# Attention scores of the later chunks as two full-array float32r products in place of one 64-row float32 product

## The chip, the cores and the metric

The kernel runs on one core of one Trainium2 chip. Times are device microseconds from launch to end; a kernel is judged by the median of several runs. The profiler takes one execution instruction by instruction, and its span runs from the first to the last instruction.

## What is computed

Banded attention with sink tokens, followed by a two-layer feed-forward block. The reference, cut to what matters (B=4, H=8, S=768, D=64, n_sink=4, window=128; the feed-forward block has 512 inputs and 2048 inner units):

```python
scores = scale * np.matmul(q, k.transpose(0, 1, 3, 2))
keep = is_sink | in_window            # the first 4 keys, or the last 128
scores = np.where(keep, scores, -1000000000.0)
a = np.exp(scores - np.max(scores, axis=-1, keepdims=True))
a = a / (np.sum(a, axis=-1, keepdims=True) + 1e-09)
x = np.matmul(a, v)                   # heads side by side: 3072 rows of 512
h = x @ w_in
sp = np.where(h > 20.0, h, np.log1p(np.exp(np.minimum(h, 20.0))))
g = h * np.tanh(sp)
y = g @ w_out
```

## The kernel before

The 3072 rows are cut into 12 chunks of 256 rows (two blocks of 128 queries). The four chunks that open a batch see one or two blocks of keys and come first; the other eight, the late chunks, see three blocks of keys, of which each query block uses two and 32 columns of sinks, 288 columns in all.

Attention of a chunk goes by pairs of heads (`pair`). The two heads of a pair lie on the two halves of the 128 partitions, each with its 64 dimensions as rows: `ks` holds k and `qh` holds q, transposed. For each of the two query blocks `qk` makes the scores, one float32 product for each head (L358), with 64 rows of contraction each, in PSUM tiles `att`. VectorE (DVE) adds the mask and takes the minimum (L365), ScalarE (ACT) exponentiates (L368), the sums give `rc` (L371 to L373), the rows are normalised on ACT (L379) or DVE (L378), TensorE (PE) transposes them (L389, L398 for the sinks), copies bring them to SBUF (`pth`, `psk`, `sks`), and PE multiplies them with v (L407, 64 output columns for each head, and L411 for the sinks). The result is split into a float32r part and a float32r rest (`w`).

The feed-forward block goes by steps, eight for each chunk and 96 in all (`step`). A step takes two of the 16 blocks of inner units: 24 products of 256 columns (L446, tile `hp`; each float32 product is made of three float32r products of high and low parts), a chain on ACT and DVE (L454 to L459), a copy to the high part `gh` (L247) and a subtraction for the low part `gl` (L258 on GpSimd, which the profile calls POOL, or L260 on DVE), and 12 products of 512 columns (L474, tile `acc`; eight read `gh`, four `gl`). The weights come as float64 and are split into float32r parts by DVE, ACT and POOL in the first 190 us.

The order of every engine's instructions is fixed beforehand. Each piece of work is added to a plan with a rank, a price on each engine that can do it, and the buffers that it takes; `solve` lets the plan run in a model and picks engine and place, and `emit` writes the instructions in that order. Where the model leaves PE without work, `emit` puts products of zeros (L569). Copies go to ACT or DVE (`copy_ways`), subtractions to POOL or DVE (`sub_ways`), loads to SyncE's queue, SP (`load`). Buffers have tags with a number of places: `raw` 3 (the weights as they come), `w` 81, `ks` and `qh` 2 each.

Of the kernel before, what the change touches and what calls it, by code (L numbers as in the profile page):

```python
# [14 lines left out]
F32R = mybir.dt.float32r  # L15
# [6 lines left out]
B, H, S, D = 4, 8, 768, 64  # L22
DM, DF = 512, 2048
P = 128
NBLK = S // P
SK = 32
PITCH = P + SK
# [4 lines left out]
TB = 2  # L32
T = TB * P
# [7 lines left out]
PE, ACT, DVE, POOL, SP = "pe", "act", "dve", "pool", "sp"  # L41
# [8 lines left out]
LEAD, LEADG, LEADN = 11, (20, 14, 8), 9  # L50
WARM, SPARE, ROOM = 14, 250, 4
ZERO = 224
SH, QUICK = 1.0, 2
LOWS = {"wi": "dpppdpdddddddddd", "wo": "dppppppppppddddd"}


def f32(ap):
    return ap.bitcast(F32)
# [19 lines left out]
def pe_t(*ns):  # L78
    return sum(n / 2.4 + 13.3 for n in ns)
# [24 lines left out]
class Plan:  # L104
# [6 lines left out]
    def add(self, prio, ways, deps=(), bufs=(), new=()):  # L111
        deps = {id(d): d for d in list(deps) + [b.maker for b in bufs] if d is not None}
        t = Task(prio, ways, list(deps.values()), list(bufs) + list(new), list(new))
        for b in t.bufs:
            b.users += 1
        for b in new:
            b.maker = t
        self.tasks.append(t)
        return t
# [104 lines left out]
class Fast(Base):  # L224
# [82 lines left out]
    def operands(self, b, c3, pr, rank, pre):  # L307

        i0 = TB * c3
        first = c3 == 0  # L310
        nb = 2 if first else 3
        j0 = 0 if first else i0 - 1
        w = nb * PITCH - SK
        if pre:
            ks, qh, vt = (Buf(None, None) for _ in range(3))
            ks.t, qh.t, vt.t = pre
            return (ks, qh, vt, [], []), None, []
        ks, qh, vt = Buf("ks", [P, 3 * PITCH - SK]), Buf("qh", [P, T]), Buf("vt", [P, 2, 3, D])
        hs = slice(2 * pr, 2 * pr + 2)
        ldk = [self.load(rank, ks, lambda: ks.t[:, 0:w], self.k[b, pr, :, j0 * PITCH:j0 * PITCH + w], w / 2),  # L320
               self.load(rank, qh, lambda: qh.t, self.q[b, pr, :, i0 * P:i0 * P + T], T / 2)]
        ldv = [self.load(rank + 1, vt, lambda: vt.t[:, :, 0:nb, :], self.v[b, hs, :, j0:j0 + nb, :].rearrange("h p j d -> p h j d"), nb * 64)]
        if first:
            return (ks, qh, vt, ldk, ldv), None, []
        vr = Buf("vsr", [P, TB, P])
        return (ks, qh, vt, ldk, ldv), vr, [self.load(rank + 1, vr, lambda: vr.t, self.vs[b, pr], 128)]

    def pair(self, b, c3, pr, rank, x, x_done):


        nc, add = self.nc, self.plan.add
        first = c3 == 0
# [6 lines left out]
        for i in range(TB):  # L339
            r = rank + i  # L340
            nm, sm, rc = Buf("nm", [P, 2]), Buf("sm", [P, 2]), Buf("rc", [P, 2])
            if not first:
                n, mask, c0 = W2, self.m2, i * PITCH
            elif i == 0:
                n, mask, c0 = P, self.m0, 0
            else:
                n, mask, c0 = 2 * P, self.m1, 0
            st = [Buf("att", [P, n]) for _ in range(2)]

            def mov(rows, n=n, c0=c0):  # L350
                if n == 2 * P:
                    return ks.t[rows, 0:2 * PITCH].rearrange("p (a c) -> p a c", c=PITCH)[:, :, 0:P]
                return ks.t[rows, c0:c0 + n]

            def qk(st=st, mov=mov, i=i):
                for e in range(2):
                    rows = slice(e * D, (e + 1) * D)
                    yield nc.tensor.matmul(st[e].t, qh.t[rows, i * P:(i + 1) * P], mov(rows), start=True, stop=True)  # L358
            s = add(r, {PE: (2 * (n / 1.2 + 106) + 100, qk)}, ldk, [ks, qh], st)
            ex = []  # L360
            for e in range(2):
                new = ([p2] if i == 0 else []) + [nm, sm] if e == 0 else []
# [2 lines left out]
                a = add(r + .03 + .01 * e, {DVE: (dve_t(n) + 8, lambda st=st, pv=pv, nm=nm, e=e, mask=mask, n=n: nc.vector.tensor_tensor_reduce(  # L365
                    out=pv(), in0=st[e].t[:, 0:n], in1=mask, scale=-0.125, scalar=BIG, op0=ALU.add, op1=ALU.min, accum_out=nm.t[:, e:e + 1]))},
                    [s], [st[e]] + old, new)
                a = add(r + .05 + .01 * e, {ACT: (act_t(n, ptr=2), lambda pv=pv, nm=nm, sm=sm, e=e: nc.scalar.activation(  # L368
                    pv(), pv(), AF.Exp, bias=nm.t[:, e:e + 1], scale=-1.0, accum_out=sm.t[:, e:e + 1]))}, [a], [p2, nm, sm])
                ex.append(a)  # L370
            a = add(r + .07, {ACT: (act_t(2), lambda rc=rc, sm=sm: nc.scalar.activation(rc.t, sm.t, AF.Copy, bias=1e-9), 0, PEN_N),  # L371
                              DVE: (72, lambda rc=rc, sm=sm: nc.vector.tensor_scalar(rc.t, sm.t, 1e-9, None, ALU.add))}, ex, [sm], [rc])
            a = add(r + .08, {DVE: (84, lambda rc=rc: nc.vector.reciprocal(rc.t, rc.t))}, [a], [rc])  # L373
# [9 lines left out]
            cols = (0, PITCH) if not first else ((None, 0) if i == 0 else (0, P))  # L383
# [6 lines left out]
            a = add(r + OTP, {PE: (109 * (2 if cols[0] is None else 4), tr)}, norm, [p2], [pt])  # L390
# [4 lines left out]
        if not first:  # L395
            psk = Buf("psk", [P, 2 * TB, SK])
            a = add(rank + 1.11, self.copy_ways(P, lambda: psk.t, lambda: p2.t.rearrange("p i e c -> p (i e) c")[:, :, P:PITCH]), norms, [p2], [psk])
            a = add(rank + OTP + 1.02, {PE: (109, lambda: nc.tensor.transpose(ssk.t, psk.t.rearrange("p a c -> p (a c)"), self.ident))}, [a], [psk], [ssk])  # L398
            last.append(add(rank + OTP + 1.09, self.copy_ways(P, lambda: sks.t, lambda: ssk.t, True), [a], [ssk], [sks]))
        r = rank + TB + OVP  # L400
# [439 lines left out]
```

## Time and profile before

| | |
|---|---|
| median of 3 runs | 762.6 us (762.48 to 765.71) |
| the profiled execution | 764.29 us, its span 762.5 us |
| busy PE / ACT / DVE / POOL | 746.5 / 553.6 / 418.4 / 111.7 us |
| granted TensorE clock | 0.995 on the mean |
| moved by DMA | 52.62 MB |

Busy is the time in which an engine has an instruction running; for PE this takes in loading and emptying between two products, so a full PE is not yet a PE at its peak. A float32 product shows as two records, a float32r product as one. The share of an engine is an average over stages: in the first 190 us ACT and DVE split weights, later they serve attention and the chain of the steps alone.

### The profile page before, as it was taken

Reading aid. Unit: us, or ns where it says so; the run is one execution under the profiler, and the core shown is the slowest. Engines: PE = TensorE matmul, PEld = TensorE weight load, DVE = VectorE, ACT = ScalarE, POOL = GpSimd, SP = SyncE. Lnnn points to the kernel's source line nnn. Section 1 sums busy time; section 2 is a strip of 40 time slices with the busy share of each in tenths; the row PEclk is TensorE's granted clock in tenths of the full one; section 3 lists DMA queues with packets and bytes.
Section 4 is the critical chain, followed back from the end, with each engine's and each line's share of the span. In section 5 each row is a group of like instructions: output and inputs, shape, how many; then the busy total and the mean of one; then the engine's idle time right before and its main releaser. Section 6 shows DMA issues by size and latency. Waiting matters only on the chain.

```text
span 762.5 us, 13564 instructions
## 1 busy us (share of the span) xinstructions
PE 746.5 (98%) x5042; PEld 618.1 (81%) x5042; DVE 418.4 (55%) x1195; ACT 553.6 (73%) x1224; POOL 111.7 (15%) x91
## 2 busy tenths in 40 slices
PE   7989999999999999999999999999999999999996
PEld 5767888788878778887788888888887888788995
DVE  6899999997555544355543434343444434443322
ACT  5899998787675677766667777777777777775653
POOL 0454422221100002100000211111021112020000
PEclk9999999999999999999999999999999999999998
DMA  6554344440221113112212212111211311100000
GB/s 191 162 162 130 119 129 129 121 120 8 85 83 49 37 46 93 37 37 73 66 37 64 62 48 65 37 57 54 65 37 41 97 37 37 65 18 1 28 1 33
DMA packets 39771, 52.62 MB, mean 69 GB/s; under 512 B 3856, under 2 KB 32528, under 8 KB 39696
## 3 DMA queue, kind: packets, MB, share of 16 engines
q1 hardware_dynamic: 39696, 51.66, 22.4%
q8 instruction: 42, 0.69, 0.4%
q14 instruction: 33, 0.27, 0.1%
HBM read 45.35 MB, written 6.29 MB: 68 GB/s over the span
## 4 chain that ended last, share of the span: by engine, by line
PE 80%; ACT 11%; DVE 4%; DMA 2%; issue 1%; ACTq 0%; DVEq 0%
PE acc L474 30%; PE hp L446 30%; PE att L358 6%; PE att L407 5%; PE att L389 4%; PE att L411 3%; ACT p L368 2%; PE att L446 2%; ACT p L379 1%; ACT w L247 1%; ACT w L279 1%; DMA raw<-w_out 1%; ACT pth L247 1%; ACT u L458 1%; ACT u L457 1%; ACT u L456 1%
## 5 line engine op out<-in xcount | busy, mean ns | idle before, releaser
L446 PE MATMUL hp<-w,w 128*128 128x256 f32 x2208 | 302.5, 288 | 0.8 <-DVE n L459 0.6
L446 PEld LDWEIGHTS hp<-w,w 128*128 128x128 f32 x2208 | 277.2, 191 | 17.8 <-issue 11.4
L474 PE MATMUL acc<-w,gh 128*128 128x512 f32 x768 | 198.8, 396 | 0.0
L474 PEld LDWEIGHTS acc<-w,gh 128*128 128x128 f32 x768 | 136.4, 189 | 29.1 <-issue 5.9
L258 POOL TENSOR_TENSOR gl<-n,gh 128x512 fp32r<-128x512 f32 x46 | 59.4, 1292 | 445.5 <-ACT gh L247 371.3
L459 DVE SCALAR_TENSOR_TENSOR n<-u,hp 128x512 f32<-128x512 f32 x92 | 62.8, 684 | 98.4 <-ACT u L458 98.1
L455 DVE TENSOR_SCALAR u<-u 128x512 f32<-128x512 f32 x96 | 41.6, 433 | 124.2 <-ACT u L454 124.1
L474 PE MATMUL acc<-w,gl 128*128 128x512 f32 x384 | 107.9, 395 | 0.0
L368 ACT ACTIVATE p<-p,nm 128x288 f32<-128x288 f32 (+1 forms) x192 | 95.2, 497 | 16.7 <-DVE nm L365 16.7
L247 ACT ACTIVATE gh<-n 128x512 fp32r<-128x512 f32 x94 | 59.3, 631 | 54.3 <-DVE n L459 54.1
L456 ACT ACTIVATE u<-u,bias 128x512 f32<-128x512 f32 x96 | 69.3, 723 | 38.8 <-DVE u L455 38.8
L454 ACT ACTIVATE u<-hp 128x512 f32<-128x512 f32 x92 | 54.7, 595 | 46.1 <-PE hp L446 44.1
L474 PEld LDWEIGHTS acc<-w,gl 128*128 128x128 f32 x384 | 70.8, 188 | 14.3 <-DVE gl L260 0.3
L365 DVE CUSTOM_DVE_ANT_0 p<-att,m 128x288 f32<-128x288 f32 (+1 forms) x192 | 74.6, 419 | 2.9 <-PE att L358 1.7
L457 ACT ACTIVATE u<-u,bias 128x512 f32<-128x512 f32 x96 | 69.0, 720 | 2.2
L358 PE MATMUL att<-ks,qh 64*128 64x288 f32 (+2 forms) x376 | 66.6, 431 | 0.0
L379 ACT ACTIVATE p<-p,rc 128x288 f32<-128x288 f32 (+2 forms) x105 | 50.4, 497 | 19.1 <-DVE rc L373 19.1
L389 PE MATMUL att<-ident,p 128*128 128x128 f32 x352 | 56.0, 276 | 5.5 <-ACT p L379 2.0
L458 ACT ACTIVATE u<-u 128x512 f32<-128x512 f32 x96 | 59.9, 625 | 1.7
L358 PEld LDWEIGHTS att<-ks,qh 64*128 64x128 f32 x376 | 28.5, 186 | 27.7 <-issue 24.2
L389 PEld LDWEIGHTS att<-ident,p 128*128 128x128 f32 x352 | 41.2, 140 | 11.1 <-ACT p L379 3.6
L260 DVE TENSOR_TENSOR gl<-n,gh 128x512 fp32r<-128x512 f32 x50 | 36.3, 727 | 22.9 <-PE acc L474 12.7
(78 smaller groups left out, 664.7 us busy)
## 6 DMA issues: line engine op xcount, KB each, us to landing
raw<-w_in SPq DMA_DIRECT2D x16, 512.0 KB, 3.7
raw<-w_out SPq DMA_DIRECT2D x16, 512.0 KB, 4.2
ks<-k_p SPq DMA_DIRECT2D x32, 224.0 KB, 2.5
y<-u SPq DMA_DIRECT2D x24, 256.0 KB, 2.1
vt<-v_b SPq DMA_DIRECT2D x32, 192.0 KB, 3.3
qh<-q_p SPq DMA_DIRECT2D x47, 128.0 KB, 2.5
vsr<-v_s SPq DMA_DIRECT2D x32, 128.0 KB, 3.0
ks<-k_p SPq DMA_DIRECT2D x15, 144.0 KB, 2.1
```

The source lines that it names most:

```text
L247: ways[ACT] = act_t(n, psum), lambda: nc.scalar.activation(dst(), src(), AF.Copy, scale=scale or 1.0)
L258: ways[POOL] = pool_t(n), lambda: nc.gpsimd.tensor_tensor(dst(), a(), b(), ALU.subtract)
L358: yield nc.tensor.matmul(st[e].t, qh.t[rows, i * P:(i + 1) * P], mov(rows), start=True, stop=True)
L365: a = add(r + .03 + .01 * e, {DVE: (dve_t(n) + 8, lambda st=st, pv=pv, nm=nm, e=e, mask=mask, n=n: nc.vector.tensor_tensor_reduce(out=pv() ...
L368: a = add(r + .05 + .01 * e, {ACT: (act_t(n, ptr=2), lambda pv=pv, nm=nm, sm=sm, e=e: nc.scalar.activation(pv(), pv(), AF.Exp, bias=nm.t[: ...
L389: yield nc.tensor.transpose(pt.t[:, e, x * P:(x + 1) * P], p2.t[:, i, e, cols[x]:cols[x] + P], self.ident)
L446: yield nc.tensor.matmul(hp.t[:, y, :], w_.t[:, fs], x_.t[:, kt % 2, :], start=kt == 0 and n_ == 0, stop=kt == KT - 1 and n_ == 2)
L456: a = add(r + .52, {ACT: (act_t(N, ptr=1), lambda: nc.scalar.activation(u.t, u.t, AF.Square, bias=self.one))}, [a], [u])
L457: a = add(r + .53, {ACT: (act_t(N, ptr=1), lambda: nc.scalar.activation(u.t, u.t, AF.Ln, bias=self.half, scale=0.5))}, [a], [u])
L458: a = add(r + .54, {ACT: (act_t(N), lambda: nc.scalar.activation(u.t, u.t, AF.Exp, scale=-1.0))}, [a], [u])
L459: e = add(r + .55, {DVE: (dve_t(N), lambda: nc.vector.scalar_tensor_tensor(m.t, u.t, 1.0, hp.t, ALU.subtract, ALU.mult))}, [a], [u, hp], [m])
L474: yield nc.tensor.matmul(acc[t].t, g_.t[:, y, ts_], w_.t, start=new and n_ == 0, stop=done)
```

## The change

In the late chunks (`not first`) the scores are made from float32r parts. A new function, `halves`, loads k of each head twice, once onto partitions 0 to 63 and once onto 64 to 127, with the two heads side by side in the columns (tile `raw`, 2 x 448 columns), and q in the same way (tile `w`, 2 x 256 columns). A copy rounds k to float32r on all 128 partitions; a subtraction puts the rest of k on the lower 64. For q a copy makes the rounded part `qa` and a subtraction the rest `qb`, both on all 128 partitions. So one product of `qa` with `ks` over 128 rows holds two of the four terms, one of `qb` with `ks` the other two, and they add up in PSUM: two products for each head, four for each query block. Loads have rank 3 below the pair's, as before; the splitting comes 1.5 later (`SPL`).

```diff
--- before.py
+++ after.py
@@ -50,6 +50,7 @@
 LEAD, LEADG, LEADN = 11, (20, 14, 8), 9
 WARM, SPARE, ROOM = 14, 250, 4
 ZERO = 224
+SPL = 1.5
 SH, QUICK = 1.0, 2
 LOWS = {"wi": "dpppdpdddddddddd", "wo": "dppppppppppddddd"}
 
@@ -315,15 +316,40 @@
             ks, qh, vt = (Buf(None, None) for _ in range(3))
             ks.t, qh.t, vt.t = pre
             return (ks, qh, vt, [], []), None, []
-        ks, qh, vt = Buf("ks", [P, 3 * PITCH - SK]), Buf("qh", [P, T]), Buf("vt", [P, 2, 3, D])
+        vt = Buf("vt", [P, 2, 3, D])
         hs = slice(2 * pr, 2 * pr + 2)
+        if not first:
+            vr = Buf("vsr", [P, TB, P])
+            ks, qh, deps = self.halves(b, j0, i0, w, pr, rank)
+            ldv = [self.load(rank + 1, vt, lambda: vt.t, self.v[b, hs, :, j0:j0 + nb, :].rearrange("h p j d -> p h j d"), nb * 64)]
+            return (ks, qh, vt, deps, ldv), vr, [self.load(rank + 1, vr, lambda: vr.t, self.vs[b, pr], 128)]
+        ks, qh = Buf("ks", [P, 2 * PITCH]), Buf("qh", [P, T])
         ldk = [self.load(rank, ks, lambda: ks.t[:, 0:w], self.k[b, pr, :, j0 * PITCH:j0 * PITCH + w], w / 2),
                self.load(rank, qh, lambda: qh.t, self.q[b, pr, :, i0 * P:i0 * P + T], T / 2)]
         ldv = [self.load(rank + 1, vt, lambda: vt.t[:, :, 0:nb, :], self.v[b, hs, :, j0:j0 + nb, :].rearrange("h p j d -> p h j d"), nb * 64)]
-        if first:
-            return (ks, qh, vt, ldk, ldv), None, []
-        vr = Buf("vsr", [P, TB, P])
-        return (ks, qh, vt, ldk, ldv), vr, [self.load(rank + 1, vr, lambda: vr.t, self.vs[b, pr], 128)]
+        return (ks, qh, vt, ldk, ldv), None, []
+
+    def halves(self, b, j0, i0, w, pr, rank):
+
+
+        nc, add = self.nc, self.plan.add
+        kr, ks = Buf("raw", [P, 2, w]), Buf("raw", [P, 2, w], F32R)
+        qr, qa, qb = Buf("w", [P, 2, T]), Buf("w", [P, 2, T], F32R), Buf("w", [P, 2, T], F32R)
+        qr.brief = qa.brief = qb.brief = True
+        heads = lambda src: src.rearrange("(e d) s -> d e s", e=2)
+        up, low = slice(0, D), slice(D, P)
+
+        def twice(buf, src, kb):
+            one = self.load(rank, buf, lambda: buf.t[up], heads(src), kb)
+            return [one, self.plan.add(rank + .01, {SP: (460, lambda: nc.sync.dma_start(buf.t[low], heads(src)), 2000 + kb * 2.9)}, [], [buf])]
+        ldk = twice(kr, self.k[b, pr, :, j0 * PITCH:j0 * PITCH + w], w / 2)
+        ldq = twice(qr, self.q[b, pr, :, i0 * P:i0 * P + T], T / 2)
+        r = rank + SPL
+        a = add(r, self.copy_ways(2 * w, lambda: ks.t, lambda: kr.t), ldk, [kr], [ks])
+        k = add(r + .02, self.sub_ways(2 * w, lambda: ks.t[low], lambda: kr.t[low], lambda: f32(ks.t[low])), [a], [kr, ks])
+        a = add(r + .01, self.copy_ways(2 * T, lambda: qa.t, lambda: qr.t), ldq, [qr], [qa])
+        q = add(r + .03, self.sub_ways(2 * T, lambda: qb.t, lambda: qr.t, lambda: f32(qa.t)), [a], [qr, qa], [qb])
+        return ks, (qa, qb), [k, q]
 
     def pair(self, b, c3, pr, rank, x, x_done):
 
@@ -352,11 +378,17 @@
                     return ks.t[rows, 0:2 * PITCH].rearrange("p (a c) -> p a c", c=PITCH)[:, :, 0:P]
                 return ks.t[rows, c0:c0 + n]
 
-            def qk(st=st, mov=mov, i=i):
+            def qk(st=st, mov=mov, i=i, c0=c0, n=n):
+                cols = slice(i * P, (i + 1) * P)
                 for e in range(2):
                     rows = slice(e * D, (e + 1) * D)
-                    yield nc.tensor.matmul(st[e].t, qh.t[rows, i * P:(i + 1) * P], mov(rows), start=True, stop=True)
-            s = add(r, {PE: (2 * (n / 1.2 + 106) + 100, qk)}, ldk, [ks, qh], st)
+                    if first:
+                        yield nc.tensor.matmul(st[e].t, qh.t[rows, cols], mov(rows), start=True, stop=True)
+                    else:
+                        for n_, part in enumerate(qh):
+                            yield nc.tensor.matmul(st[e].t, part.t[:, e, cols], ks.t[:, e, c0:c0 + n], start=n_ == 0, stop=n_ == 1)
+            cost = 2 * (n / 1.2 + 106) + 100 if first else pe_t(*[n] * 4)
+            s = add(r, {PE: (cost, qk)}, ldk, [ks, qh] if first else [ks, *qh], st)
             ex = []
             for e in range(2):
                 new = ([p2] if i == 0 else []) + [nm, sm] if e == 0 else []
```

What this does to the order, at three places. `L389` of the kernel after is the new product; its other lines are those of before, moved: L439 is the product with v (L407 before), L443 that of the sinks (L411), L478 is L446, L506 is L474, L486 to L490 are L454 to L458, L248 is the copy (L247), L266 and L344 are loads.

PE, the second query block of a pair in a late chunk. Before:

```order
L474 MATMUL acc_0_5840<-w_0_1395,gl_0_5974 128x512
L358 MATMUL att_0_6021<-ks_0_5693,qh_0_5698 128x288
L358 MATMUL att_1_6022<-ks_0_5693,qh_0_5698 128x288
L407 MATMUL att_0_6028<-pth_0_5921,vt_0_5713 64x256 x2
L407 MATMUL att_0_6028<-pth_0_5921,vt_0_5713 64x128 x4
L411 MATMUL att_0_6028<-sks_0_6002,vsr_0_5718 128x128 x2
L446 MATMUL hp_0_6050<-w_0_5036,w_0_1675 128x256
```

After:

```order
L506 MATMUL acc_0_6107<-w_0_1395,gl_0_6256 128x512
L389 MATMUL att_0_6300<-raw_0_5952,w_0_5922 128x288
L389 MATMUL att_0_6300<-raw_0_5952,w_0_5927 128x288
L389 MATMUL att_1_6301<-raw_0_5952,w_0_5922 128x288
L389 MATMUL att_1_6301<-raw_0_5952,w_0_5927 128x288
L439 MATMUL att_0_6307<-pth_0_6189,vt_0_5971 64x256 x2
L439 MATMUL att_0_6307<-pth_0_6189,vt_0_5971 64x128 x4
L443 MATMUL att_0_6307<-sks_0_6279,vsr_0_5976 128x128 x2
L478 MATMUL hp_0_6328<-w_0_5241,w_0_1675 128x256
```

The four products stand where the two stood, between the last product with `gl` and the product with v. Of the 64 scores of the late chunks, 26 stand between L474 and L446 before, 15 inside a group of L474, 22 between L474 and L407, and one between two L446; after, one of the 15 has moved to stand between L446 and L474. The products of zeros are 164 before and after.

ACT, the copy to `gh` in a step of the same stage. Before:

```order
L454 ACTIVATE u_0_5931<-hp_0_5883 128x512
L456 ACTIVATE u_0_5931<-u_0_5931,bias 128x512
L457 ACTIVATE u_0_5931<-u_0_5931,bias 128x512
L458 ACTIVATE u_0_5931<-u_0_5931 128x512
L247 ACTIVATE gh_0_5964<-n_0_5951 128x512
L368 ACTIVATE p_2566_0_5960,sm_2_5962<-p_2566_0_5960,nm_1_5961 128x288 x2
L247 ACTIVATE pth_0_5921<-att_0_5976 128x2x256
L379 ACTIVATE p_2566_0_5960<-p_2566_0_5960,rc_0_5989 128x288
```

After:

```order
L486 ACTIVATE u_0_5915<-hp_0_5858 128x512
L488 ACTIVATE u_0_5915<-u_0_5915,bias 128x512
L489 ACTIVATE u_0_5915<-u_0_5915,bias 128x512
L490 ACTIVATE u_0_5915<-u_0_5915 128x512
L248 ACTIVATE raw_0_5952<-raw_0_5810 128x896
L248 ACTIVATE gh_0_5959<-n_0_5954 128x512
L400 ACTIVATE p_2539_0_5873,sm_1_5957<-p_2539_0_5873,nm_0_5956 128x288 x2
L411 ACTIVATE p_2539_0_5873<-p_2539_0_5873,rc_0_5986 128x288 x2
```

The copy of k (128x896) has come between the last exponential of a step and the copy to `gh`. All 32 copies of k are on ACT, and 17 of the 32 copies of q; 15 of q are on DVE. ACT has 25 normalisations of 128x288 more than before and nine copies to `pth` less; DVE the reverse. The subtractions for k (64x896) are 21 on POOL and 11 on DVE, those for q 8 on POOL and 24 on DVE; of those for `gl`, POOL has 22 (46 before) and DVE 74 (50).

SP, the loads of late pairs, with what they wait for. Before:

```order
L265 DMA ks_0_6886<-k_p 128x448 [waits DMAHW7_49,PE_49]
L265 DMA qh_0_6891<-q_p 128x256 [waits DMAHW0_49]
L265 DMA vt_0_6906<-v_b 128x2x192 [waits DMAHW1_49,PE_49]
L265 DMA vsr_0_6910<-v_s 128x256 [waits DMAHW2_49,PE_49]
L265 DMA ks_0_7053<-k_p 128x448 [waits DMAHW3_49,PE_49]
L265 DMA qh_0_7058<-q_p 128x256 [waits DMAHW4_49]
L265 DMA vt_0_7073<-v_b 128x2x192 [waits DMAHW5_49,PE_49]
L265 DMA vsr_0_7078<-v_s 128x256 [waits DMAHW6_49,PE_49]
```

After:

```order
L266 DMA vt_0_5786<-v_b 128x2x192 [waits DMAHW5_49,PE_49]
L266 DMA vsr_0_5790<-v_s 128x256 [waits DMAHW6_49,PE_49]
L266 DMA raw_0_5810<-k_p 64x2x448 [waits DMAHW4_49,DMAHW7_49,DMAHW3_49,Pool_49]
L344 DMA raw_0_5810<-k_p 64x2x448 [waits DMAHW0_49]
L266 DMA w_0_5845<-q_p 64x2x256 [waits DMAHW1_49,DVE_49]
L266 DMA w_0_5849<-q_p 64x2x256 [waits DMAHW2_49,DVE_49]
L344 DMA w_0_5845<-q_p 64x2x256
L344 DMA w_0_5849<-q_p 64x2x256
L266 DMA vt_0_5971<-v_b 128x2x192 [waits DMAHW5_49,PE_49]
L266 DMA vsr_0_5976<-v_s 128x256 [waits DMAHW6_49,PE_49]
```

A late pair loads k in two DMAs of 64 partitions where it loaded it in one of 128, and q likewise, two pairs of q at a time. The load of k now waits for POOL, which last read the buffer, where it waited for PE.

## The prediction

> **What bounds the kernel now.** First the page's busy times and its granted clock, then the same by stretches of 60 us, then who TensorE (PE) waited for.
>
> ```profile
> PE 746.5 (98%) x5042; PEld 618.1 (81%) x5042; DVE 418.4 (55%) x1195; ACT 553.6 (73%) x1224; POOL 111.7 (15%) x91
> PEclk9999999999999999999999999999999999999998
> ```
>
> ```profile
> 120.00:180.00 60.00, 58.19 (x374) 50.74 (x373) 55.92 (x110) 47.92 (x94) 13.73 (x10) 1.00 0.34 104
> 180.00:240.00 60.00, 60.00 (x398) 50.12 (x398) 36.31 (x100) 38.42 (x82) 3.88 (x3) 1.00 0.18 57
> ...
> 480.00:540.00 60.00, 60.00 (x414) 49.86 (x413) 24.99 (x77) 44.67 (x100) 9.07 (x7) 1.00 0.19 56
> ```
>
> ```profile
> PE att L389 <- ACT p L379: 2.0, 4, 1.4
> ```
>
> In the stretches the columns are window, length, then busy us (and instructions) of PE, weight loads, DVE, ACT and POOL, then clock, DMA share, GB/s. From 180 us on PE is busy for all 60 of 60 us at full clock, while ACT has 15 us of every 60 free, DVE 35 and POOL 51. PE's largest wait on anybody is 2.0 us in the whole run. So what is taken from PE in the late stage comes out of the span, and what is put on the others is free until it reaches an instruction that PE waits for. All 64 scores that the edit touches belong to the eight late chunks.
>
> **What one such score costs PE now.** "Busy" does not tell it, because PE also counts as busy while it loads weights or empties. I read it from starts in the timeline of PE: start, duration, instruction, count.
>
> ```profile
> 565.09 1.07 PE L474 MATMUL acc<-w,gl 128*128 128x512 f32 x4
> 566.08 0.76 PE L358 MATMUL att<-ks,qh 64*128 64x288 f32 x4
> 566.77 2.42 PE L446 MATMUL hp<-w,w 128*128 128x256 f32 x18
> 569.02 0.60 PE L389 MATMUL att<-ident,p 128*128 128x128 f32 x4
> 569.46 0.27 PE L398 MATMUL att<-ident,psk 128*128 128x128 f32 x1
> ...
> 570.28 2.00 PE L474 MATMUL acc<-w,gh 128*128 128x512 f32 x8
> 572.12 1.07 PE L474 MATMUL acc<-w,gl 128*128 128x512 f32 x4
> 573.12 0.76 PE L358 MATMUL att<-ks,qh 64*128 64x288 f32 x4
> 573.81 1.09 PE L407 MATMUL att<-pth,vt 128*64 128x256 f32 x12
> ...
> 578.68 1.55 PE L474 MATMUL acc<-w,gh 128*128 128x512 f32 x6
> ```
>
> The same neighbours without a score between them stand near the end of the run (first three rows), and once ahead of the output product L407 (next two); the last four rows are a score in the middle of a group of L474:
>
> ```profile
> 714.27 2.00 PE L474 MATMUL acc<-w,gh 128*128 128x512 f32 x8
> 716.11 1.07 PE L474 MATMUL acc<-w,gl 128*128 128x512 f32 x4
> 717.02 3.04 PE L446 MATMUL hp<-w,w 128*128 128x256 f32 x24
> 719.89 0.40 PE L474 MATMUL acc<-w,gh 128*128 128x512 f32 x1
> ...
> 694.71 1.07 PE L474 MATMUL acc<-w,gl 128*128 128x512 f32 x4
> 695.71 1.09 PE L407 MATMUL att<-pth,vt 128*64 128x256 f32 x12
> ...
> 320.56 0.63 PE L474 MATMUL acc<-w,gh 128*128 128x512 f32 x2
> 321.12 0.76 PE L358 MATMUL att<-ks,qh 64*128 64x288 f32 x4
> 321.80 1.66 PE L474 MATMUL acc<-w,gh 128*128 128x512 f32 x6
> 323.30 1.09 PE L474 MATMUL acc<-w,gl 128*128 128x512 f32 x4
> ```
>
> Undisturbed, 24 float32r products of 256 columns take 719.89 - 717.02 = 2.87 us, 0.1196 each, and 12 of 512 columns 717.02 - 714.27 = 2.75 us, 0.229 each.
> - A, between L474 and L446: the four gl products take 0.99 in place of 0.91 us until the score starts (+0.08), the score 0.69, and the 18 products after it 2.25 in place of 18 x 0.1196 = 2.15 (+0.10): 0.87 us.
> - B, inside L474: 323.30 - 320.56 = 2.74 us, less the eight gh products alone, 716.11 - 714.27 = 1.84: 0.90 us.
> - C, ahead of L407: from gl to L407 573.81 - 572.12 = 1.69 us, and 695.71 - 694.71 = 1.00 without a score: 0.69 us. L407 writes 64 columns and pays for its own entry either way.
>
> The pure streaming in this is smaller. L389 is float32 on the whole array: four records in 569.46 - 569.02 = 0.44 us, 0.11 for 128 columns. For 288 columns that makes 0.248; a float32 product is two records, and the two heads run side by side on 64 rows each: 0.495 us. The rest, 0.2 to 0.4 us, is loading and emptying at the edges of the 64-row form.
>
> **The change on PE.** A score becomes four float32r products of 288 columns on the whole array, the form of L446 and L474. By a straight line between 0.1196 (256) and 0.229 (512), 288 columns cost 0.133; four cost 0.533. From those forms into one another the rows above show no extra edge (0.91 us for the four gl ahead of L446), so I take none. I save 0.34 us in A, 0.37 in B, 0.16 in C. In the order of instructions A occurs 27 times (one of these between two L446), B 15, C 22; the new order keeps the neighbours of all but one. 27 x 0.34 + 15 x 0.37 + 22 x 0.16 = 9.2 + 5.5 + 3.5 = 18.2 us. Bounds for the unseen 288-column form: proportional to 512 columns 0.129, to 256 columns 0.135, so four cost 0.516 to 0.538, which moves the sum by +1.1 or -0.3 us. The zero products that fill PE's gaps (L569) stay 164.
>
> A rule of the Trainium skill speaks against this: TensorEngine Tiling (Array Packing), section Theoretical Speedup, gives a contraction of 64 rows or less up to twice the speed when two tiles share the array, and the change gives that packing up. The rows agree that the heads overlap; by that rule, which counts streaming alone, nothing would be gained; it is the first rival, priced there.
>
> **What it adds elsewhere.** Rows by form:
>
> ```profile
> L247 ACT ACTIVATE gh<-n 128x512 fp32r<-128x512 f32 x94 | 59.3, 631 | 54.3 <-DVE n L459 54.1
> L247 ACT ACTIVATE psk<-p 128x128 f32<-128x128 f32 x25 | 7.8, 310 | 0.8
> L258 POOL TENSOR_TENSOR gl<-n,gh 128x512 fp32r<-128x512 f32 x46 | 59.4, 1292 | 445.5 <-ACT gh L247 371.3 <-PE hp L446 50.0 <-PE att L411 24.1
> L260 DVE TENSOR_TENSOR gl<-n,gh 128x512 fp32r<-128x512 f32 x50 | 36.3, 727 | 22.9 <-PE acc L474 12.7 <-ACT gh L247 8.8 <-issue 0.8
> L379 ACT ACTIVATE p<-p,rc 128x288 f32<-128x288 f32 x60 | 31.5, 534 | 17.1 <-DVE rc L373 17.0
> L378 DVE TENSOR_SCALAR p<-p,rc 128x288 f32<-128x288 f32 x68 | 24.5, 372 | 2.0
> ```
>
> ACT gets all 32 copies of k (128x896). The line through 310 (128) and 631 ns (512) gives 0.95 us: 30.4 us. It gets 17 of the 32 copies of q (0.63 each: 10.7) and 25 more normalisations (0.534 each: 13.4), and loses nine 512-wide copies to DVE (about 0.6 each: -5) and eight tiny ones: about +48 us in some 500, so from 44.7 to about 50 busy us of 60. POOL gets 21 of the 32 subtractions of k (64x896): between 1.29 us, if half the rows made up for the width, and 1.292 x 896/512 = 2.26; I take 2.26, since no row shows a price that falls with rows; and eight of q, less 24 of gl: about +27 us. DVE takes those 24 gl at 0.727, the other 11 of k and 24 of q, and copies, less 25 normalisations of 0.372: about +50 us. None of the three fills up in the late stage, so I cost this at nothing, and the cover is this:
>
> ```profile
> 567.49 0.63 ACT L247 ACTIVATE gh<-n 128x512 fp32r<-128x512 f32 x1 [0.81 <-DVE n L459]
> 574.80 0.63 ACT L247 ACTIVATE gh<-n 128x512 fp32r<-128x512 f32 x1 [0.81 <-DVE n L459]
> ```
>
> In the new order the copy of k stands on ACT right ahead of a copy to gh, where ACT now idles 0.81 us for DVE. If it pushes gh by its whole 0.95 us, PE still is not late: gh ends at 568.12 and 575.43, and L474 reads it at 570.28 and 578.68, slacks of 2.2 and 3.2 us. A copy of q (0.63) in the same step still fits. The k copy's own wait is for its load; on the queue of loads (SP) this waits for POOL's subtraction one pair earlier. A pair takes about 15.4 us (two steps); less 0.95, 2.26 and a landing, it is there some 9 us early.
>
> ```profile
> 300.40 0.33 SPq L265 DMA_DIRECT2D ks<-k_p  x1
> ...
> ks<-k_p SPq DMA_DIRECT2D x32, 224.0 KB, 2.5
> qh<-q_p SPq DMA_DIRECT2D x47, 128.0 KB, 2.5
> ```
>
> The split loads make four DMAs of two: 64 more issues of about 0.33 us on SP, and k and q twice over, 32 x 352 KB = 11.5 MB on 52.6, at a DMA share of 0.19. Nothing stands behind them but loads that are as early. The copy of k stands two copies to gh, or steps, ahead of its score in nearly all pairs (one in four of them).
>
> The exception is the seam between 160 and 240 us, where DVE has 4 us of 60 free and the last weights are still split. Conversions of the first late pairs fall there (one ahead of the last weights). Were four of them exposed by 0.95 on ACT and 0.727 on DVE, it would cost 6.7 us; hidden, nothing; reordering could also gain something. I take 0.6, near the hidden end, since PE is full from 180 us on.
>
> **Sum.** 18.2 - 0.6 = 17.6 us off the profiled execution: 764.3 - 17.6 = 746.7 (its span 762.5 to 744.9). That execution lay 1.7 us above the median of 762.6, so the median should go to 745.0.
>
> **Rivals.**
> - *Only streaming counts (no change).* If the 0.2 to 0.4 us at the edges belong to the change of data or to semaphore waits, not to the 64 rows, they stay. Then 0.533 replaces 0.495: 64 x 0.038 = +2.4 us, 765.0. Against it: L446 into L474 and back shows no edge though these wait on semaphores too, nor does float32 L389. 5%.
> - *Half of it.* The four new products overlap their weight loads, but edges of 0.08 and 0.10 remain. A and B save 0.16 to 0.19, C nothing: about 7 us, 755.5. 7%.
> - *ACT hands gh over late (slower).* Two more ACT operations in a pair, 0.95 + 0.63 us, on an engine that then is 84% busy. Were all of it on the path, 32 x 1.58 = 50 us: 795. It decides from 18.2/32 = 0.57 us of exposed wait in each pair, that is gh delayed by over 2.7 us in a step. For it: gh stands directly behind the k copy; against it: the slacks. 4%.
> - *The seam costs its whole 6.7 us:* 751. 2%.
>
> **How the numbers follow.** The forecast has 82%. Differences under 0.5% (3.8 us) cannot be told from none. Faster: 82 + 7 + 2 = 91%; same 5%; slower 4%. The range goes from 742 (18.2 + 1.1 us, nothing lost at the seam, and another 1.3 for rounding of the starts) to 752 (the seam at its worst); half of it and worse lie outside.
>
> **What would show it.** In the new profile a score should read as four records of 128x288 on 128 rows with about 0.53 us to the next line's start, 18 L446 products behind it should take 2.15 us, not 2.25, and PE should stay at 60 of 60 in the late stretches. Wrong would be a start-to-start near 0.7 us (edges), or waits of L474 for gh on ACT (slower). A POOL row of 64x896 near 1.3 or 2.3 us tells which end held.

## The result and the profile after

The kernel after takes 744.22 us (median of four runs, 743.74 to 744.32) against 762.54 us for the kernel before (median of four, 761.06 to 765.71): a ratio of 0.9753, 95% interval 0.9722 to 0.9784. The difference of the medians is 18.3 us.

The lines of the page that answer to those of before: busy time of each engine (share, instructions), and the granted clock of PE in 40 slices.

```profile
PE 728.5 (98%) x5042; PEld 638.5 (86%) x5042; DVE 474.0 (64%) x1258; ACT 585.4 (79%) x1284; POOL 136.4 (18%) x96
PEclk9999999999999999999999999999999999999999
```

The same stretches of 60 us (busy us and instructions of PE, weight loads, DVE, ACT, POOL; then clock, DMA share, GB/s):

```profile
120.00:180.00 60.00, 58.90 (x386) 51.70 (x385) 56.28 (x110) 48.33 (x94) 14.10 (x11) 1.00 0.35 105
180.00:240.00 60.00, 60.00 (x407) 52.31 (x406) 42.41 (x109) 46.33 (x101) 6.36 (x4) 1.00 0.35 97
...
480.00:540.00 60.00, 60.00 (x423) 54.09 (x422) 33.59 (x92) 49.00 (x104) 12.35 (x7) 1.00 0.31 80
```

PE still does 5042 instructions and is still busy for all of 60 us in the late stage. It now gets through 423 instructions in the window from 480 us on, where it got through 414. ACT is busy 49.0 us of that window instead of 44.7, DVE 33.6 instead of 25.0, POOL 12.4 instead of 9.1. So the late stage has stayed limited by PE, and PE needs less time for as many instructions.

What a score costs now is read from starts, as before. The timeline of PE in the kernel after (start, duration, instruction, count), at a score between L506 (L474 before) and L478 (L446), and at one ahead of L439 (L407). L389 is the new product.

```profile
548.59 1.07 PE L506 MATMUL acc<-w,gl 128*128 128x512 f32 x4
549.50 0.69 PE L389 MATMUL att<-raw,w 128*128 128x288 f32 x4
550.02 2.30 PE L478 MATMUL hp<-w,w 128*128 128x256 f32 x18
552.16 0.60 PE L421 MATMUL att<-ident,p 128*128 128x128 f32 x4
...
555.26 1.07 PE L506 MATMUL acc<-w,gl 128*128 128x512 f32 x4
556.17 0.70 PE L389 MATMUL att<-raw,w 128*128 128x288 f32 x4
556.80 1.09 PE L439 MATMUL att<-pth,vt 128*64 128x256 f32 x12
```

And one in the middle of a group of L506:

```profile
313.39 0.63 PE L506 MATMUL acc<-w,gh 128*128 128x512 f32 x2
313.86 0.69 PE L389 MATMUL att<-raw,w 128*128 128x288 f32 x4
314.38 1.54 PE L506 MATMUL acc<-w,gh 128*128 128x512 f32 x6
315.76 1.07 PE L506 MATMUL acc<-w,gl 128*128 128x512 f32 x4
```

By the prediction's own three readings:

- A: four gl products take 549.50 - 548.59 = 0.91 us until the score starts, what they take undisturbed. The score takes 550.02 - 549.50 = 0.52 us. The 18 products behind it take 552.16 - 550.02 = 2.14 us, and 18 x 0.1196 = 2.15 undisturbed. Cost 0.52 us (0.87 before).
- B: 315.76 - 313.39 = 2.37 us, less 1.84 for the eight gh products alone: 0.53 us (0.90 before).
- C: 556.80 - 555.26 = 1.54 us, less the 1.00 without a score: 0.54 us (0.69 before).

The 128x288 record's duration of 0.69 us says little: before, 64-row scores read 0.76 us, and the cost differs by up to 0.37. It has to be read from starts, and over the neighbours too.

The two profiled executions differ by more than the medians, 764.3 to 743.7 us. 1.5 us of that lay in the first 62 us, where the granted clock (the third number from the end) was 0.97 in before and 1.00 in after. The first window of before, and then of after:

```profile
0.00:60.00 60.00, 52.63 (x408) 37.49 (x409) 49.88 (x200) 48.20 (x152) 22.36 (x24) 0.97 0.57 173
```

```profile
0.00:60.00 60.00, 54.20 (x414) 38.38 (x414) 50.25 (x206) 49.25 (x154) 23.21 (x24) 1.00 0.59 175
```

Counting the products of L474 (L506 after) in both traces, before reaches the first at 64.1 us and the 241st at 194.6, after at 62.6 and 193.1: the lead is 1.5 us ahead of the last weights and behind them. From there to the 1009th (of 1152) before takes 498.2 us and after 479.1. The gain of the change falls in the late chunks.

### The profile page after: what moved, and what is told of

It is laid out like the page before. It is cut to its first block, busy times and chain, and to the rows that moved or that the text cites. A ratio compares the mean times of both kernels' runs of the same rounds, so it can differ in the third digit from the quotient of the medians.

```text
span 741.4 us, 13855 instructions
## 1 busy us (share of the span) xinstructions
PE 728.5 (98%) x5042; PEld 638.5 (86%) x5042; DVE 474.0 (64%) x1258; ACT 585.4 (79%) x1284; POOL 136.4 (18%) x96
## 4 chain that ended last, share of the span: by engine, by line
PE 82%; ACT 12%; DVE 3%; DMA 1%; issue 0%; ACTq 0%
PE acc L506 32%; PE hp L478 30%; PE att L439 5%; PE att L389 5%; PE att L421 4%; PE att L443 3%; ACT p L400 2%; ACT p L411 2%; PE att L478 2%; ACT w L280 2%; ACT w L248 1%; DMA raw<-w_out 1%; ACT pth L248 1%; ACT u L490 1%; ACT raw L290 1%; ACT u L489 1%
## 5 line engine op out<-in xcount | busy, mean ns | idle before, releaser
L478 PE MATMUL hp<-w,w 128*128 128x256 f32 x2208 | 299.7, 286 | 0.9 <-DVE n L491 0.8
L478 PEld LDWEIGHTS hp<-w,w 128*128 128x128 f32 x2208 | 277.6, 190 | 7.5 <-DVE n L491 1.9
L506 PE MATMUL acc<-w,gh 128*128 128x512 f32 x768 | 197.2, 394 | 0.0
L506 PEld LDWEIGHTS acc<-w,gh 128*128 128x128 f32 x768 | 136.8, 189 | 23.6 <-issue 0.5
L506 PE MATMUL acc<-w,gl 128*128 128x512 f32 x384 | 107.6, 395 | 0.0
L400 ACT ACTIVATE p<-p,nm 128x288 f32<-128x288 f32 (+1 forms) x192 | 95.3, 497 | 12.4 <-DVE nm L397 12.3
L487 DVE TENSOR_SCALAR u<-u 128x512 f32<-128x512 f32 x96 | 44.2, 461 | 74.7 <-ACT u L486 74.5
L506 PEld LDWEIGHTS acc<-w,gl 128*128 128x128 f32 x384 | 70.8, 188 | 14.4 <-DVE gl L261 0.3
L248 ACT ACTIVATE gh<-n 128x512 fp32r<-128x512 f32 x93 | 58.2, 626 | 27.9 <-DVE n L491 27.6
L411 ACT ACTIVATE p<-p,rc 128x288 f32<-128x288 f32 (+2 forms) x129 | 61.2, 502 | 23.0 <-DVE rc L405 22.5
L259 POOL TENSOR_TENSOR raw<-raw,raw 64x896 fp32r<-64x896 f32 x21 | 44.5, 2121 | 169.3 <-ACT raw L248 107.0
L486 ACT ACTIVATE u<-hp 128x512 f32<-128x512 f32 x92 | 54.3, 590 | 25.2 <-PE hp L478 24.7
L261 DVE TENSOR_TENSOR gl<-n,gh 128x512 fp32r<-128x512 f32 x74 | 52.5, 710 | 26.5 <-ACT gh L248 13.5
L490 ACT ACTIVATE u<-u 128x512 f32<-128x512 f32 x96 | 60.0, 626 | 1.7
L421 PE MATMUL att<-ident,p 128*128 128x128 f32 x352 | 55.6, 275 | 2.9 <-DVE rc L404 1.3
L259 POOL TENSOR_TENSOR gl<-n,gh 128x512 fp32r<-128x512 f32 x22 | 29.2, 1329 | 152.7 <-ACT gh L248 114.8
L439 PE MATMUL att<-pth,vt 128*64 128x128 f32 (+1 forms) x504 | 47.9, 322 | 0.4 <-ACT pth L248 0.2
```

The costliest lines, as they stand in the source:

```text
L248: ways[ACT] = act_t(n, psum), lambda: nc.scalar.activation(dst(), src(), AF.Copy, scale=scale or 1.0)
L259: ways[POOL] = pool_t(n), lambda: nc.gpsimd.tensor_tensor(dst(), a(), b(), ALU.subtract)
L411: ACT: (act_t(n, ptr=1), lambda row=row, rc=rc, e=e: nc.scalar.activation(row(), row(), AF.Copy, scale=rc.t[:, e:e + 1]), 0, PEN_N),
L421: yield nc.tensor.transpose(pt.t[:, e, x * P:(x + 1) * P], p2.t[:, i, e, cols[x]:cols[x] + P], self.ident)
L439: yield nc.tensor.matmul(o.t[e * D:(e + 1) * D, o0:o1], vt.t[:, e, j, :], pth.t[:, e, c0:c1], start=n_ == 0, stop=first and n_ == len(jobs ...
L478: yield nc.tensor.matmul(hp.t[:, y, :], w_.t[:, fs], x_.t[:, kt % 2, :], start=kt == 0 and n_ == 0, stop=kt == KT - 1 and n_ == 2)
```

## The experiments

All kernels but the one before are built from the kernel after; each ratio is against runs of the kernel before on the same chip.

### Is it the 64-row form, or the type of the data?

The change does two things to a score at once: float32 becomes float32r, and 64 rows become 128. The first two kernels do one each.

**Full rows, float32.** The loads still put k and q on both halves of the rows, but nothing is split: one float32 product per head over 128 rows sums every term twice, and the scale is halved.

```diff
-                        for n_, part in enumerate(qh):
-                            ... part.t[:, e, cols], ks.t[:, e, c0:c0 + n], start=n_ == 0, stop=n_ == 1)
+                        for n_, part in enumerate(qh):          # qh holds q alone, float32
+                            ... part.t[:, e, cols], ks.t[:, e, c0:c0 + n], start=True, stop=True)
-                    ... scale=-0.125
+                    ... scale=-0.125 if first else -0.0625
```

> The scores of the late chunks stay float32, but on the whole array: k and q lie on both halves of the partitions as loaded, one float32 product of 128 rows for each head sums the score twice, and the mask step halves its scale. Nothing is split. Theory (the gain came from leaving the 64-row form, whose edges cost 0.2 to 0.4 us a score): four float32 records of 288 columns at 0.248 us one after another, 0.99 us and no edge, 0.46 us above the kernel after, 64 x 0.46 = 30 us: 774 us. Rival (the edges belong to float32, and float32r took them away): they stay, 42 x 0.375 + 22 x 0.19 = 20 us more: 794 us.

Measured: 772.54 us (772.28 to 772.99), ratio 1.0142 [1.0125, 1.0159]. Its timeline of PE, a score ahead of the product with v (L433) and one ahead of the weights' product (L472):

```profile
561.34 1.07 PE L500 MATMUL acc<-w,gl 128*128 128x512 f32 x4
562.25 1.13 PE L383 MATMUL att<-raw,w 128*128 128x288 f32 x4
563.31 1.09 PE L433 MATMUL att<-pth,vt 128*64 128x256 f32 x12
...
570.03 1.07 PE L500 MATMUL acc<-w,gl 128*128 128x512 f32 x4
570.94 1.13 PE L383 MATMUL att<-raw,w 128*128 128x288 f32 x4
571.69 2.52 PE L472 MATMUL hp<-w,w 128*128 128x256 f32 x18
574.05 0.60 PE L415 MATMUL att<-ident,p 128*128 128x128 f32 x4
```

On full rows the four gl products take 0.91 us in both places (562.25 - 561.34, 570.94 - 570.03): no edge on the way in. The next line's start alone would mislead here: at 571.69 it gives 0.75 us for the score, and the 18 products then take 2.36 in place of 2.15. Over both the score costs 574.05 - 570.94 - 2.15 = 0.96 us ahead of L472, and 563.31 - 561.34 - 1.00 = 0.97 ahead of L433, the same in both places: four records of 0.24 us, the rate that the prediction read from float32 on the whole array (0.11 us for 128 columns, 0.248 for 288). So a full-array score has one price wherever it stands, and the 64-row score of before had two (0.87 and 0.69). The time is 10.8 us over the kernel before on the same chip: four float32 records one after the other (0.96) cost more than two pairs side by side with their edges, by 0.09 us in each of the 27 scores of A and the 15 of B (from 320.54 to 323.37, 2.83 us here and 2.74 before) and by 0.28 in each of the 22 of C, 9.9 us together.

**64 rows, float32r.** All four terms as in the kernel after, but each as a product of 64 rows per head, the heads side by side; single loads, hi and lo in the same rows.

```diff
+                if not first:
+                    for n_ in range(4):
+                        for e in range(2):
+                            rows = slice(e * D, (e + 1) * D)
+                            yield nc.tensor.matmul(st[e].t, qh[n_ // 2].t[rows, cols], ks.t[rows, n_ % 2, c0:c0 + n], start=n_ == 0, stop=n_ == 3)
+                    return
```

> The scores of the late chunks are float32r with all four terms, but in the 64-row form, the two heads side by side: eight products of 64 rows for each score in place of four of 128. Theory (edges of the 64-row form): streaming 0.53 us as in the kernel after, plus edges of about 0.375 us next to whole-array products and 0.19 us ahead of the product with v: 42 x 0.375 + 22 x 0.19 = 20 us above the kernel after: 764 us, no better than before. Rival (float32r itself took the edges away): 744 to 747 us.

Measured: 765.60 us (765.22 to 767.72), ratio 1.0058 [1.0039, 1.0077]. Its timeline of PE:

```profile
566.65 1.07 PE L502 MATMUL acc<-w,gl 128*128 128x512 f32 x4
567.65 0.80 PE L381 MATMUL att<-raw,w 64*128 64x288 f32 x8
568.38 2.42 PE L474 MATMUL hp<-w,w 128*128 128x256 f32 x18
570.63 0.60 PE L417 MATMUL att<-ident,p 128*128 128x128 f32 x4
...
573.73 1.07 PE L502 MATMUL acc<-w,gl 128*128 128x512 f32 x4
574.73 0.80 PE L381 MATMUL att<-raw,w 64*128 64x288 f32 x8
575.46 1.09 PE L435 MATMUL att<-pth,vt 128*64 128x256 f32 x12
```

The edges are back, with the new data type: the gl products take 1.00 us (+0.09), the score 0.73, the 18 products 2.25 (+0.10), 0.92 us in all; ahead of L435 it costs 575.46 - 573.73 - 1.00 = 0.73. The row form makes them. The same four terms cost 0.92 us in this form and 0.52 in that of the kernel after.

The Trainium skill's page TensorEngine Tiling (Array Packing), section Key Properties, says that changing the tiling mode drains the engine. The trace agrees: 0.08 to 0.10 us are lost at each end of a 64-row score among the weights' products, and nothing where all rows are used.

### What does the added work cost by itself?

**The splitting done, and not used.** Scores of before, with their own loads of k and q, and beside them all loads, copies and subtractions of the kernel after, whose results nothing reads.

```diff
+            k2, q2, deps = self.halves(b, j0, i0, w, pr, rank)
+            ks, qh = Buf("ks", ...), Buf("qh", [P, T])
+            deps += [self.load(rank, ks, ...), self.load(rank, qh, ...)]
+            self.idle = [k2, *q2]
```

> The scores are those of before (64 rows, float32), and besides them all the loads, copies and subtractions of the kernel after are done, and every score waits for them; nothing reads their result. Theory (the split work is wholly hidden behind a full TensorE): 762.5 us, within 2 us of before. Rival (the split work costs something in the stage where weights are still split, or by delaying gh): 3 to 7 us more, 766 to 769 us.

Measured: 762.66 us (median of ten, 761.99 to 764.68) against 761.77 (median of 13) before, ratio 1.0014 [1.0005, 1.0024]: 1.1 us (0.4 to 1.8) for all of it. Its windows at the seam and late:

```profile
120.00:180.00 60.00, 58.81 (x384) 51.59 (x383) 56.16 (x111) 48.22 (x94) 13.83 (x11) 1.00 0.38 111
...
480.00:540.00 60.00, 60.00 (x412) 50.41 (x409) 31.38 (x91) 47.80 (x103) 12.33 (x7) 1.00 0.38 104
```

PE stays at 60 of 60 late, with ACT, DVE and POOL nearly as loaded as in the kernel after and the DMA share at 0.38, above its 0.31. The cover that the prediction relied on is there. Where the 1.1 us lie the traces don't show: from the first output product to the last the two profiled executions take 691.4 us here and 691.8 before.

### How much cover is left?

**The copies twice.** Every copy of k and of q is done twice over; nothing else.

```diff
+        a = add(r + .004, self.copy_ways(2 * w, lambda: ks.t, lambda: kr.t), [a], [kr, ks])
...
+        a = add(r + .014, self.copy_ways(2 * T, lambda: qa.t, lambda: qr.t), [a], [qr, qa])
```

> The kernel after with each of its two copies (k and q) done twice, one behind the other: about 1.6 us more in a pair, on ACT or DVE. Theory (hidden, gh has 2 to 3 us of slack in a step): 744 to 746 us. Rival (ACT at 49 of 60 us is near its end and hands gh over late): more than half of 32 x 1.58 = 50 us shows, 770 us or more.

Measured: 754.12 us (753.80 to 754.61), ratio 0.9902 [0.9886, 0.9919], some 10 us more than the kernel after, and neither of the two expectations. The late window does not explain it, for PE has no gap in it and no other engine is full:

```profile
480.00:540.00 60.00, 60.00 (x426) 54.14 (x425) 36.62 (x91) 50.09 (x108) 5.38 (x4) 1.00 0.30 80
```

The waits of PE do (who waited for whom, us in total, times, longest):

```profile
PE acc L508 <- ACT gh L248: 5.6, 3, 2.7
```

Two stops of 2.7 us, in the same kind of step, and one of 0.25. The second long one is followed here on four engines; the timelines of POOL, DVE, ACT and PE of this kernel (in brackets the idle time ahead and what ended it):

```profile
611.37 2.13 POOL L259 TENSOR_TENSOR raw<-raw,raw 64x896 fp32r<-64x896 f32 x1 [5.85 <-DMA vsr<-v_s]
613.57 1.62 POOL L259 TENSOR_TENSOR w<-w,w 128x512 fp32r<-128x512 f32 x1
```

```profile
611.49 2.56 DVE L261 TENSOR_TENSOR gl<-n,gh 128x512 fp32r<-128x512 f32 x1 [0.35 <-ACT gh L248]
613.97 1.25 DVE L406 TENSOR_SCALAR rc<-sm 128x2 f32<-128x2 f32 x1
...
622.21 0.69 DVE L261 TENSOR_TENSOR gl<-n,gh 128x512 fp32r<-128x512 f32 x1
```

```profile
615.65 0.96 ACT L413 ACTIVATE p<-p,rc 128x288 f32<-128x288 f32 x2 [2.30 <-DVE rc L407]
...
621.40 0.61 ACT L248 ACTIVATE gh<-n 128x512 fp32r<-128x512 f32 x1
```

```profile
622.06 1.50 PE L508 MATMUL acc<-w,gh 128*128 128x512 f32 x3 [2.72 <-ACT gh L248]
```

DVE's subtraction for gl, 0.69 us at 622.21, takes 2.56 us at 611.49, because POOL began its subtraction of k 0.12 us earlier: 611.37 + 2.13 = 613.50, and gl ends 0.55 us after that. POOL's next subtraction, of q, ends at 613.57 + 1.62 = 615.19, and rc, 0.17 us undisturbed, takes 1.25 beside it and ends at 615.22. The normalisation on ACT waits 2.30 us for rc; the copy to gh stands behind that on ACT; PE stands still for 2.72 us. With the copies doubled, gl stands ahead of rc in DVE's order here (rc ahead of gl in the kernel after), and POOL's subtraction begins just ahead of it. The other long stop goes the same way (gl 2.55 us, rc 1.25, ACT's wait 2.29).

The meeting alone does not stop PE. In two more steps, from 531.6 and 594.8 us on, gl takes 2.6 us beside POOL and ACT waits 2.4 us for rc; behind the second PE stops for 0.25 us, behind the first not at all. There ACT idles for 1.3 us more between the normalisation and the next copy to gh. In the steps of the long stops ACT has two copies of 512 columns and two exponentials more on that way, and idles for 0.06 us.

Counting output products as above, the profiled execution is 2.5 us behind that of the kernel after at 541 us (1.9 of them from the first 64 us, at a clock of 0.97) and 10.7 at 654 us. So some 8 us belong to the stops and to a lower clock behind the last of them (see the end); what was lost at the start does not.

**The copies twice, and no subtraction of k or q on POOL.** This tells ACT's load from the meeting of DVE and POOL: ACT keeps its doubled copies.

```diff
-        k = add(r + .02, self.sub_ways(2 * w, ..., lambda: f32(ks.t[low])), [a], [kr, ks])
+        k = add(r + .02, self.sub_ways(2 * w, ..., lambda: f32(ks.t[low]), (DVE,)), [a], [kr, ks])
...                                            # and the same for q
```

> The kernel with both copies done twice, but all its subtractions for k and q on DVE and none on POOL. In the run with the copies twice, PE waited for gh twice for 2.7 us, and in the window before such a wait a DVE subtraction of 0.69 us took 2.6 us while POOL subtracted k for 2.1 us beside it. Theory (DVE and POOL keep each other out, and that made gh late, not the load of ACT): the waits go, 744 to 747 us. Rival (ACT is simply too full with the copies twice): the waits stay, 752 to 756 us.

Measured: 743.62 us (742.16 to 744.16), ratio 0.9751 [0.9727, 0.9776], against 0.9753 for the kernel after: all of the 10 us are gone. Its late window, to be held against the one above:

```profile
480.00:540.00 60.00, 60.00 (x423) 54.11 (x422) 37.37 (x100) 51.18 (x109) 2.59 (x2) 1.00 0.31 80
```

ACT is busier than in the kernel that stopped (51.18 us against 50.09), DVE too (37.37 against 36.62). DVE's order is the same, the doubled copy, gl, rc; its timeline here:

```profile
543.90 0.69 DVE L261 TENSOR_TENSOR gl<-n,gh 128x512 fp32r<-128x512 f32 x1 [0.35 <-ACT gh L248]
544.50 0.17 DVE L406 TENSOR_SCALAR rc<-sm 128x2 f32<-128x2 f32 x1
544.70 1.09 DVE L261 TENSOR_TENSOR raw<-raw,raw 64x896 fp32r<-64x896 f32 x1
```

gl takes 0.69 us after the same 0.35 of waiting for gh, and rc 0.17. So the doubled copies alone stop nothing; it took the meeting of DVE and POOL, in a step that left ACT hardly any idle time. The two plans also differ elsewhere: in this step ACT does one of the two normalisations here and both in the kernel that stopped. ACT's wait for rc makes 2.30 of the 2.72 us; whether the other 0.4 come from the meeting is not shown.

**The kernel after, with the same subtractions on DVE alone** asks whether such meetings cost the kernel after anything.

> The kernel after with all its subtractions for k and q on DVE and none on POOL, the copies done once. Theory (in the kernel after, DVE and POOL keep each other out in places that nothing waits for, and PE is full): 743.5 to 744.5 us, no difference. Rival (collisions cost the kernel after something as well): 741 us or less.

Measured: 745.25 us (five runs, 744.33 to 745.58), ratio 0.9778 [0.9765, 0.9792]. It is no faster; the interval meets that of the kernel after. It does not take the meetings away, though: POOL has 51 of the subtractions for gl here (22 in the kernel after), and beside them rc takes up to 1.03 us. What a kernel without any such meeting would take is not tested. In the kernel after, DVE is held up behind 19 of the 21 subtractions of k on POOL, but at another instruction than gl. DVE's rc, which takes 0.17 us undisturbed, there:

```profile
484.92 0.68 DVE L404 TENSOR_SCALAR rc<-sm 128x2 f32<-128x2 f32 x1
```

and POOL at the same time:

```profile
483.46 2.11 POOL L259 TENSOR_TENSOR raw<-raw,raw 64x896 fp32r<-64x896 f32 x1 [5.02 <-issue]
```

483.46 + 2.11 = 485.57, and rc ends at 485.60. Half a microsecond is lost on DVE, and PE waits for nothing after 200 us in this kernel.

### Would more scores gain more?

**The fourth chunk of the first stage too**, in the new form (the same edit, for chunks with one key block less, where the weights are still being split).

```diff
+        if first and b == 3:
+            ks, qh, deps = self.halves(b, j0, i0, w, pr, rank)
...
+        full = not first or (b == 3)
```

> The scores of the fourth chunk (one or two key blocks, the last of those that open a batch) made in the new form too; its work falls at about 120 to 190 us, beside the last weights. Theory (the new form pays only where PE is full and the others have room; here DVE is busy 56 of 60 us): 8 scores save about 0.25 us each, 2 us, but four pairs of splits of about 2.5 us on ACT and DVE are exposed: 746 to 752 us. Rival (it pays wherever a 64-row score stands): 742 us.

Measured: 758.50 us (median of eight, 756.77 to 760.33), ratio 0.9952 [0.9932, 0.9972], 14 us more than the kernel after. The products of zeros, which the plan puts where its model leaves PE without work (in groups by line: busy us, mean ns), in the kernel after:

```profile
L601 PE MATMUL acc<-zero 128*128 128x224 bf16 x164 | 21.0, 272 | 0.0
```

and here:

```profile
L612 PE MATMUL acc<-zero 128*128 128x224 bf16 x245 | 30.4, 268 | 0.0
```

81 more of them, 54 of these between 120 and 240 us: there the plan has no work for PE, and a cheaper score gives nothing. By the count of output products this kernel is 1.9 us behind the kernel after at the 145th (144.6 us) and 12.8 at the 241st (206.0 us), so most of the loss falls there.

**Chunks two to four of the first stage too** (`b > 0`).

> The scores of the second, third and fourth chunk made in the new form too; their work falls into the first 190 us, where ACT is busy 58 of 60 us and DVE 55. Theory: 24 scores save about 6 us on PE, which waits there anyway, and twelve pairs of splits of 2 to 3 us on the two full engines are exposed: 760 to 780 us. Rival (it pays wherever a 64-row score stands): 738 us.

Measured: 786.45 us (784.60 to 787.97), ratio 1.0312 [1.0284, 1.0340]. 506 products of zeros, and PE waits for the splitting itself:

```profile
PE att L400 <- DVE raw L261: 5.4, 3, 3.4
```

**The splitting of the fourth chunk, not used**: the kernel after, with only the loads, copies and subtractions of that chunk added, beside its old scores.

> The kernel after, and for the fourth chunk the loads, copies and subtractions of the split besides its old float32 scores, which wait for them; nothing reads the parts. Theory (the split work of the fourth chunk, put beside the last weights, costs the 14 us by which the run with the fourth chunk in the new form lay above the kernel after): 757 to 761 us, within 2 us of that run. Rival (the new products or their place in the order cost it): 744 to 748 us.

Measured: 759.97 us (median of ten, 758.95 to 762.28), ratio 0.9969 [0.9956, 0.9982], about as slow as with the scores in the new form. So the added work, with the wait for it, costs the time, not the form of the product. The splitting of 32 pairs cost 1.1 us where PE was the limit; that of four more costs some 16 us here. Whether it is DVE, busy for 56.3 of 60 us between 120 and 180 us in the kernel after already, or the buffers that its data hold is not told apart: no run gives the parts buffers of their own.

## Why the prediction was right

The forecast was 745.0 us (742 to 752); 744.22 was measured. By its steps:

- *The edges belong to the 64-row form, and go with it.* Shown from both sides: float32 on full rows has no edge (0.91 us for gl, 0.96 to 0.97 in both places), float32r on 64 rows has them again (+0.09, +0.10). The rival in which only streaming counts (765.0) and the one of half the gain (755.5) are out for the kernel after; four terms of 64 rows, which keep the edges, come out at 765.6.
- *The price of the unseen product, 0.133 us for 288 columns.* From the score's start to the next line's it is 0.52 us in A, which makes 0.130 each: within the bounds (0.129 to 0.135).
- *A, B and C.* The savings measured 0.35, 0.37 and 0.15 us, for 0.34, 0.37 and 0.16. With the counts, 27 x 0.35 + 15 x 0.37 + 22 x 0.15 = 9.5 + 5.6 + 3.3 = 18.3 us; the medians differ by 18.3. That the two agree to a tenth is luck. Over the whole stretch at once A saves 0.36 (569.02 - 565.09 = 3.93 us before, 552.16 - 548.59 = 3.57 after), which makes 18.6, and the profiled executions differ by 19.1 us from the 241st output product on. What makes up the rest is not shown.
- *0.6 us at the seam.* The traces' lead is 1.5 us ahead of it and behind it, so it cost nothing that can be seen; the splitting beside the old scores cost 1.1 us (0.4 to 1.8) over the whole run. The 0.6 was a choice near the hidden end and follows from no row: the size is about right, the place is not shown.
- *The median against the profiled execution.* The prediction took off the 1.7 us by which before's profiled execution lay above its median. It fits that this execution lost 1.5 us against that of the kernel after in the first 62 us, at a clock of 0.97, ahead of the scores that the change touches.
- *POOL's price.* 2.12 us for 64x896, near the upper bound (2.26): half the rows did not make up for the width. The row, with those of ACT's copy and of DVE's subtraction (count, busy us, mean ns, idle ahead):

```profile
L259 POOL TENSOR_TENSOR raw<-raw,raw 64x896 fp32r<-64x896 f32 x21 | 44.5, 2121 | 169.3 <-ACT raw L248 107.0 <-issue 54.2 <-DVE u L487 8.1
L248 ACT ACTIVATE raw<-raw 128x896 fp32r<-128x896 f32 x32 | 30.3, 946 | 3.2 <-PE att L389 2.8
L261 DVE TENSOR_TENSOR raw<-raw,raw 64x896 fp32r<-64x896 f32 x11 | 12.0, 1089 | 1.2 <-ACT raw L248 0.9
```

  POOL's total rose by 24.7 us (27 forecast), DVE's by 55.6 (50), ACT's by 31.8 (48). ACT's 49.0 us of 60 in the late window is the "about 50" of the forecast. For the run it had added up durations, and these did rise by 46.3 us (623.5 to 669.8); the busy time counts once where an instruction overlaps the one before it.
- *The rival that ACT hands gh over late.* Not in the kernel after: gh is not among PE's waits. With the copies twice it did come, in two steps of the run and not in each pair. ACT's load alone was not the cause, for it was higher in the kernel that ran without a stop.

The weak step is therefore the cover. It was worked out from busy shares and from ACT's slack of 2.2 and 3.2 us ahead of gh, engine by engine. That POOL holds DVE up was not in it. In the kernel after POOL's subtraction falls on rc, for about 0.5 us, and the slack holds that. With the copies done twice it fell on gl, for 1.9 us, and in the two steps with a long stop a second one fell on rc, for 1.1; these stops and the low clock behind one of them cost some 8 us. That the plan of the kernel after set POOL's subtraction beside rc and not beside gl the prediction had not foreseen; in that it was lucky.

## What to carry to other kernels

Where PE is the limit, price a product by starts, over a stretch that takes in its neighbours, against the same neighbours without it: here a packed 64-row score among full-array products cost 0.69 to 0.90 us for 0.495 us of streaming, and one with more products, of float32r parts on all rows, cost 0.52 to 0.54. Free time on the other engines was cover where PE was full for the whole stage: there the splitting of 32 pairs cost 1.1 us, while that of four pairs cost some 16 us beside the weights, where DVE was busy for 56 of 60 us. Before work goes to POOL, look what DVE does in the same microseconds: slack must be read on the chain DVE to ACT to PE, not from busy shares.

## What the runs showed of the hardware that was not expected

- Some instructions of DVE stand still until the instruction on POOL has ended: gl 2.56 us in place of 0.69 beside POOL's 2.13, and even rc on two columns 0.68 in place of 0.17. Others do not: the subtraction w<-att,w, which reads one input from PSUM, takes 0.42 us in the kernel after whether POOL runs beside it (23 times after 200 us) or not. The Trainium skill's page SBUF — State Buffer, section Who interferes with whom, says that DVE and GpSimd share a pair of ports that only one of them holds at a time, and that a DVE instruction contends for it when it has two inputs in SBUF, or copies or scales in a two-port mode. The trace agrees for the subtractions (gl has both inputs in SBUF), and fits for rc.
- A stop of PE can cost more than its length. In the kernel with the copies twice, after the stop of 2.72 us that ended at 622.06, the granted clock was 0.57 for four microseconds:

```profile
622.00:626.00 4.00, 3.94 (x10) 3.12 (x11) 1.32 (x3) 3.44 (x8) 0.00 (x0) 0.57 0.00 0
```

  That is another 4 x 0.43 = 1.7 us, and by so much the kernel falls further behind there. After a stop of 2.68 us that ended near 559 us it stayed at full clock:

```profile
558.00:563.00 5.00, 4.11 (x24) 3.30 (x26) 1.74 (x6) 4.44 (x10) 0.00 (x0) 1.00 0.00 0
```

  Why one of two stops of nearly the same length slowed the clock stays open.
